# A fused attention and maxout kernel: the first quad by halves, one engine's copies, other stores, a new mask list and a new instruction order

## The chip, the cores and the metric

The kernel runs on one core of a Trainium2 chip. Five engines work on their own instruction streams, each in order, and wait for one another by semaphores: TensorE (PE, matrix products and transposes; its weight loads are shown apart as PEld), VectorE (DVE), ScalarE (ACT), GpSimd (POOL) and SyncE (SP), which here only issues transfers. Sixteen DMA engines carry them out. The metric is the device time of one execution in microseconds, the median of several runs; lower is better.

## What is computed

Inputs: q, k and v of 8 batches x 8 heads x 576 tokens x 64, three weights of 512 x 768 and one of 768 x 512, all float32. Only scores within tau = 0.02 of the row's maximum take part in the softmax.

```
scores = q @ k.T / sqrt(64)                       # 576 x 576 for each of 64 heads
scores = where(scores >= max(scores) - tau, scores, -1e9)
attn   = exp(scores - max(scores));  attn /= sum(attn) + 1e-9
x      = (attn @ v), heads side by side           # 4608 x 512
h      = maximum(x @ w1, x @ w2, x @ w3)          # 4608 x 768
out    = h @ w_out                                # 4608 x 512
```

## The kernel before

**Quads.** Four heads of one batch make a quad g (16 of them), held as two pairs r = 0, 1 of two heads i = 0, 1. `load` (line 181) fetches q and k with head i on partitions 64i to 64i+63, 9 tokens to a partition: the first eight tokens of both pairs in one transfer and the ninth ones in another, then v in four transfers. For the first quad alone (`first=True`) the eight-token rows come apart by pair: q on SP's queue in three transfers (pair 0, ninth tokens, pair 1), k likewise on ACT's queue. All other loads are on SP's.

**Transposes.** `transposed` (257) turns q or k of one pair on PE, ten 64 x 64 pieces for r = 0 (with the ninth tokens) and eight for r = 1, for both heads at once, into a PSUM slot. `evacuated` (234) copies the slot to `qt` (ACT, with the scale) or `kt` (DVE; ACT for pair 1 of the first quad). `swapped` (242) makes `qs`, a copy of `qt` with the partition halves exchanged, on POOL (for the first quad one of the two halves on DVE), so that both halves of PE's rows can work on the same queries.

**Scores.** A step is a quad and one of 9 chunks idx of 128 queries; each has a score product (S) for r = 0 and 1. Chunks 0 to 3 belong to head i = 0 of each pair, 5 to 8 to head 1, and chunk 4 holds the last 64 queries of both. Each S fills one of four PSUM slots, which are shared by all of PE's products.

**Softmax in two ways.** `maximum` (311) is a DVE pass that gives the row's bound. If the list `MASKED` has a 1 for the step and pair, this pass also writes z, ACT exponentiates once, and DVE removes what is under the threshold and sums (`numerators`, 331, letter k). With a 0, ACT runs twice over the scores (a Prelu with the tiny slope 2^-100, then an exponential that sums, letter n) and DVE has the maximum only. So a 1 costs DVE a pass, a 0 costs ACT one. Then DVE takes reciprocals, POOL normalizes to bf16 (`P`), and SP's queue transposes P by DMA into `ptq`.

**Products and the network.** `product` (358) multiplies `ptq` by v for one pair into `xt`; its 576 columns are copied by DVE for r = 0 and for r = 1 by ACT (512) and DVE (64). Once a batch has both its quads, `ffn` (426) runs 18 hidden products (each in two halves, F and B), of which ACT copies the first of three (`hm`) and DVE takes two maxima (`hm`, `hT`), and then the output products: two of 2 x 512 columns and one for the ninth tokens. ACT copies these to `ob` and `obr`, SP stores them. Batch 7 is done in two column parts (`SPLIT`).

**The order.** What is issued when is written out by hand in the text `ORDER`, which the loop at line 659 reads: S, T, O, F and a slot number issue PE's score products, transposes, attention products and the first halves of the network's products; B the second halves; m, e, k, n, r, p, t the maximum, exponent, the two kinds of numerators, reciprocal, normalization and DMA transpose of the next score in line; a and c the copies to `qt` and `kt`, q the swaps, x and w the copies of attention products by ACT and DVE, h, v and u those of the network; l a transfer of the next quad, y a POOL cast of v, g a load and z a cast of weights, o a store. `_Ordered` (80) ties every instruction to the one before it on its engine, so the text is each engine's order, and a wait holds back all that follows on that engine. Before the text is read, 12 warm-up transposes of the identity run on PE, and the first quad is loaded, transposed and swapped (lines 546 to 556).

## Time and profile before

| what | value |
|---|---|
| median of 3 runs | 452.66 us (452.27 to 452.84) |
| profiled execution, its own time | 451.11 us |
| its span, first to last instruction | 449.3 us |
| mean granted clock of TensorE | 0.991 |
| PE, DVE, ACT, POOL busy | 425.6, 402.0, 392.3, 314.8 us |
| chain that ended last: PE, DVE, POOL, DMA, ACT | 75%, 6%, 5%, 5%, 3% |
| first score product, first maximum | 8.08, 9.56 us |
| first network product | 67.39 us |
| last ob copy, last store issue begins | 444.29, 446.3 us |

The span leaves out 1.8 us that lie around the instructions. The profile gives for each engine the time in which it executed something; PE's is flattered, since matmuls overlap and their ends are modelled. Nearly all instructions carry line 89, the helper of `_Ordered`, so groups are told apart by the names of their tiles.

### The profile page before, as it was taken

Reading aid. Unit: us, or ns where it says so; the run is one execution under the profiler, and the core shown is the slowest. Engines: PE = TensorE matmul, PEld = TensorE weight load, DVE = VectorE, ACT = ScalarE, POOL = GpSimd, SP = SyncE. Lnnn points to the kernel's source line nnn. Section 1 sums busy time; section 2 is a strip of 40 time slices with the busy share of each in tenths; the row PEclk is TensorE's granted clock in tenths of the full one; section 3 lists DMA queues with packets and bytes.
Section 4 is the critical chain, followed back from the end, with each engine's and each line's share of the span. In section 5 each row is a group of like instructions: output and inputs, shape, how many; then the busy total and the mean of one; then the engine's idle time right before and its main releaser. Section 6 shows DMA issues by size and latency. Waiting matters only on the chain.

```text
span 449.3 us, 14063 instructions
## 1 busy us (share of the span) xinstructions
PE 425.6 (95%) x5188; PEld 314.8 (70%) x5188; DVE 402.0 (89%) x1115; ACT 392.3 (87%) x794; POOL 314.8 (70%) x416
## 2 busy tenths in 40 slices
PE   6766889999999999999999999999999999999995
PEld 6433557767688768878677867868787787787762
DVE  3999999998999999999989999999999999999541
ACT  3999999999899999999989999999999999866422
POOL 3798889989795985586776785659777787534400
PEclk8989999999999999999999999999999999999999
DMA  8989999999999999996999998999999999546622
GB/s 236 276 208 204 223 214 226 222 231 222 246 212 193 214 221 231 192 222 132 221 166 194 236 217 182 215 229 216 200 172 186 213 175 191 107 77 133 130 94 107
DMA packets 212773, 87.44 MB, mean 195 GB/s; under 512 B 185824, under 2 KB 199648, under 8 KB 212704
## 3 DMA queue, kind: packets, MB, share of 16 engines
q1 hardware_dynamic: 212144, 85.95, 93.4%
q8 instruction: 41, 0.67, 0.6%
q10 hardware_dynamic: 560, 0.59, 0.5%
q14 instruction: 28, 0.23, 0.2%
HBM read 34.60 MB, written 9.44 MB: 98 GB/s over the span
## 4 chain that ended last, share of the span: by engine, by line
PE 75%; DVE 6%; POOL 5%; DMA 5%; ACT 3%; issue 3%; SPq 1%; ACTq 0%; POOLq 0%; DVEq 0%
PE ph L89 30%; PE sc L89 26%; PE po L89 8%; PE o L89 8%; POOL P L89 3%; PE tp L89 3%; DVE z L89 3%; DVE unused L89 2%; ACT z L89 2%; DMA ptq<-P 1%; SPq L89 1%; DMA qm<-in_q_dram 1%; DMA km<-in_k_dram 1%; POOL qs L89 1%; ACT ob L89 1%
## 5 line engine op out<-in xcount | busy, mean ns | idle before, releaser
L89 POOL TENSOR_SCALAR P<-z,rs 128x576 bf16<-128x576 f32 x288 | 229.2, 811 | 89.4 <-DVE rs L89 40.6
L89 PE MATMUL sc<-kt,qs 64*128 64x256 f32 (+2 forms) x640 | 180.2, 421 | 9.2 <-ACT qt L89 3.2
L89 PE MATMUL sc<-kt,qt 64*128 64x320 f32 (+2 forms) x640 | 181.2, 432 | 4.0 <-DVE kt L89 1.2
L89 PE MATMUL ph<-xt,w 64*128 64x288 bf16 (+2 forms) x2160 | 165.0, 283 | 0.3 <-DVE hm L89 0.2
L89 PEld LDWEIGHTS <-w 64*128 64x128 bf16 (+1 forms) x2160 | 127.1, 94 | 29.4 <-issue 6.7
L89 ACT ACTIVATE z<-sc,nm 128x576 f32<-128x576 f32 x179 | 128.8, 742 | 11.6 <-DVE unused L89 9.7
L89 DVE TENSOR_SCALAR_CACHE_REDUCE unused<-sc 128x576 bf16<-128x576 f32 x179 | 130.3, 751 | 4.0 <-PE sc L89 3.4
L89 ACT ACTIVATE z<-z 128x576 f32<-128x576 f32 x179 | 121.0, 682 | 0.1
L89 PEld LDWEIGHTS sc<-kt,qs 64*128 64x128 f32 (+1 forms) x640 | 91.5, 178 | 33.3 <-ACT z L89 7.8
L89 PEld LDWEIGHTS sc<-kt,qt 64*128 64x128 f32 (+1 forms) x640 | 91.6, 177 | 21.0 <-ACT z L89 6.5
L89 DVE SCALAR_TENSOR_TENSOR z<-z 128x576 f32<-128x576 f32 x109 | 89.9, 839 | 0.3 <-ACT z L89 0.2
L89 DVE TENSOR_SCALAR_CACHE_REDUCE z<-sc 128x576 f32<-128x576 f32 x109 | 80.6, 752 | 7.4 <-PE sc L89 3.6
L89 ACT ACTIVATE z<-z,nm 128x576 f32<-128x576 f32 x109 | 81.8, 774 | 4.0 <-DVE z L89 3.4
L89 POOL COPY qs<-qt 64x640 f32<-64x640 f32 (+1 forms) x62 | 45.4, 733 | 14.7 <-ACT qt L89 11.6
L89 PE MATMUL po<-wo,hT 64*128 64x512 bf16 (+1 forms) x480 | 54.0, 356 | 0.1
L89 DVE TENSOR_TENSOR hm<-ph,hm 128x576 bf16<-128x576 f32 (+2 forms) x54 | 37.1, 687 | 12.1 <-PE ph L89 11.6
L89 ACT ACTIVATE hm<-ph 128x576 bf16<-128x576 f32 (+2 forms) x54 | 32.1, 595 | 14.9 <-PE ph L89 14.4
L89 PEld LDWEIGHTS <-hT 64*128 64x128 bf16 (+1 forms) x480 | 29.6, 97 | 16.7 <-issue 3.1
L89 DVE TENSOR_TENSOR hT<-ph,hm 128x576 bf16<-128x576 f32 (+2 forms) x54 | 37.2, 688 | 2.8
L89 PE MATMUL o<-ptq,vb 128*64 128x64 bf16 (+2 forms) x544 | 38.9, 281 | 0.2
L89 ACT ACTIVATION_READ_ACCUMULATOR z<-z 128x1 f32 x179 | 35.7, 199 | 0.0
L89 PEld LDWEIGHTS <-vb 128*64 128x64 bf16 x544 | 23.7, 111 | 14.2 <-issue 4.6
(32 smaller groups left out, 273.8 us busy)
## 6 DMA issues: line engine op xcount, KB each, us to landing
vm<-in_v_dram SPq DMA_DIRECT2D x32, 256.0 KB, 4.5
out_dram<-ob SPq DMA_DIRECT2D x32, 256.0 KB, 2.8
qm<-in_q_dram SPq DMA_DIRECT2D x15, 512.0 KB, 4.9
km<-in_k_dram SPq DMA_DIRECT2D x15, 512.0 KB, 4.7
stage<-in_moe_w_dram SPq DMA_DIRECT2D x9, 512.0 KB, 4.6
ptq<-P SPq DMA_TRANSPOSE x144, 4.1
stage<-in_moe_w_out_dram SPq DMA_DIRECT2D x3, 512.0 KB, 5.8
qm<-in_q_dram SPq DMA_DIRECT2D x16, 64.0 KB, 3.1
```

The costliest lines, as they stand in the source:

```text
L89: ins = fn(*a, **kw)
```

## The change

- The first quad is loaded by halves of the partitions: rows 0 to 63 (head 0 of each pair) first, in three transfers each of q (SP) and k (ACT's queue), the ninth tokens ahead of the rest; then rows 64 to 127, in two transfers each of q and k, all on SP. Before the text is read only head 0 is transposed, copied and swapped; the halves of head 1 become the first four T of the text, with their own a, c and q. Two filler transposes of the identity are put behind the first pair's k, and there is a thirteenth warm-up.
- In the first quad the copy of pair 1's k goes from ACT to DVE, and all swaps to POOL; the swaps are issued after the four transposes.
- `product`: for r = 1 ACT copies all 576 columns; DVE has no part in it.
- In the last batch the ninth tokens' products are copied by DVE instead of ACT, and the second store of the last 2 x 512 columns is issued on ACT's queue instead of SP's.
- `MASKED` has 102 ones of 288 instead of 109: by batch 11, 12, 11, 12, 12, 13, 12, 19, where there were 14, 9, 13, 15, 14, 13, 12, 19.
- `ORDER` is another text throughout. The number of each letter is the same but for what follows from the above: T 64 (60), a and c 32 (30), q 64 (60), k 102 (109), n 186 (179), w 16 (30). The first lines of both texts and the rest of the diff:

```diff
--- before.py
+++ after.py
@@ -22,51 +22,52 @@
 FLAT = 2.0 ** -100
 
 MASKED = """
-101000100110000110011100001010010001100010001000101000010000100000100010
-000011110101100001001001001001000001011100101011000110001010010000010011
-001010011101100000101100100001001010000110011111000001000100000110000101
-001001001101100000110001000100101000001100010011100101110110000001111111
+010000100100100010101001001100000010100011011001010000011000100000010100
+000110010101100001000011000001000010001100011010011000100000010101000100
+000111101000100010010010000100010001000110000101010100110100001101000100
+100111100100100010010000001100100000001001011110000011011110010101111100
 """
 
 
-WARM = 12
+WARM = 13
+FILL = (2, 0)
 SLOTS = 4
 SPLIT = (7,)
 ZBUFS = 4
 PBUFS = 6
 
 ORDER = """
-glllllS0lylS1mylyeS2zmlkS3lelmnlT0mS1aS2rmeqS0meqmeS3pnkT1pT0nrcaptemS0yeS1mgS2eympeS3mqtnT1S0mqnS2knrceprmS
-1epkepeS3mnyS0rkptemnS2pmnlzmS3erremtpT0empS1eklpaS2kgnS0ptnmeprrmlS1epS3mleS2pmlS0eplmetpmeS1knS3tkernkS2pt
...
+S0S1gmlS2elmgnyS3mlelT0ymeylT1kezlS2arclnT3mlnS0S1lzameT3lmeqgqrcnlT2plnpaqT1leS0qcplS3mpS2lrmT1eplmaqT0eklS
+1qnS2lmS3lepmteymeS1keqS3rnmpS2emprS1tepmnkqS3ncnprmS0elprmS1epS2megpkS0ntzS3nmntrmpemS2pemepS1kezetrmS0nmS3
...
 """
 
 
@@ -180,7 +181,7 @@
 
     def load(g, first=False):
         b, qd = quads[g]
-        L = Ls[g] = dict(b=b, qd=qd, first=first)
+        L = Ls[g] = dict(b=b, qd=qd)
         for n in "qk":
 
             L[n] = ld.tile([128, 20, D], F32, name=n + "m")
@@ -188,20 +189,28 @@
         def rows_of(src):
             return src[b, 4 * qd:4 * qd + 4].rearrange("(r i) (p c) d -> (i p) r c d", r=2, c=9)
 
-        q2 = nc.scalar if first else sync
-        srcs = (("q", q, sync), ("k", k, q2))
         if first:
-            for n, src, e in srcs:
-                e.dma_start(out=L[n][:, 0:8], in_=rows_of(src)[:, 0, 0:8])
-        for n, src, e in srcs:
-            e.dma_start(out=L[n][:, 8:10], in_=rows_of(src)[:, :, 8])
-            yield
-        for n, src, e in srcs:
-            if first:
-                e.dma_start(out=L[n][:, 10:18], in_=rows_of(src)[:, 1, 0:8])
-            else:
-                e.dma_start(out=L[n].rearrange("p (r c) d -> p r c d", r=2)[:, :, 0:8], in_=rows_of(src)[:, :, 0:8])
-            yield
+
+            for i in range(2):
+                rows = slice(64 * i, 64 * i + 64)
+                srcs = (("q", q, sync), ("k", k, sync if i else nc.scalar))
+                for n, src, e in srcs:
+                    e.dma_start(out=L[n][rows, 8:10], in_=rows_of(src)[rows, :, 8])
+                if i == 0:
+                    for r in range(2):
+                        for n, src, e in srcs:
+                            e.dma_start(out=L[n][rows, 10 * r:10 * r + 8], in_=rows_of(src)[rows, r, 0:8])
+                else:
+                    for n, src, e in srcs:
+                        e.dma_start(out=L[n].rearrange("p (r c) d -> p r c d", r=2)[rows, :, 0:8],
+                                    in_=rows_of(src)[rows, :, 0:8])
+        else:
+            for n, src in (("q", q), ("k", k)):
+                sync.dma_start(out=L[n][:, 8:10], in_=rows_of(src)[:, :, 8])
+                yield
+            for n, src in (("q", q), ("k", k)):
+                sync.dma_start(out=L[n].rearrange("p (r c) d -> p r c d", r=2)[:, :, 0:8], in_=rows_of(src)[:, :, 0:8])
+                yield
         L["vm"] = ld.tile([128, 4, 4, D], F32, name="vm")
         L["vr"] = ld.tile([128, 2, D], F32, name="vr")
         vsrc = v[b, 4 * qd:4 * qd + 4].rearrange("h (p c) d -> p h (c d)", c=9)
@@ -234,18 +243,15 @@
     def evacuated(L, n, r, dst, src):
         if n == "q":
             scalar.activation(out=dst(L["qt"]), in_=src, func=AF.Copy, scale=scale)
-        elif L["first"] and r == 1:
-            scalar.activation(out=dst(L["kt"]), in_=src, func=AF.Copy)
         else:
             vector.tensor_copy(out=dst(L["kt"]), in_=src)
 
-    def swapped(L, r):
+    def swapped(L, r, ii=(0, 1)):
 
         cols = slice(320 * r, 320 * r + 64 * (5 - r))
-        for x in range(2):
-            e = vector if x == 1 and L["first"] else pool
-            e.tensor_copy(out=L["qs"][64 * x:64 * x + 64, :, cols],
-                             in_=L["qt"][64 - 64 * x:128 - 64 * x, :, cols])
+        for x in (0, 1) if len(ii) == 2 else (1, 0):
+            pool.tensor_copy(out=L["qs"][64 * x:64 * x + 64, ii[0]:ii[-1] + 1, cols],
+                             in_=L["qt"][64 - 64 * x:128 - 64 * x, ii[0]:ii[-1] + 1, cols])
             yield
 
     def targets(L, n):
@@ -254,7 +260,7 @@
             if n == "q":
                 L["qs"] = qk.tile([128, 2, S], F32, name="qs")
 
-    def transposed(L, n, r):
+    def transposed(L, n, r, ii=(0, 1)):
 
 
         st = {}
@@ -264,7 +270,7 @@
             st["ps"] = ps = bank("tp", where)
             main = ps.rearrange("p (i z) -> p i z", i=2)[:, :, 0:256].rearrange("p i (jj u x) -> p i jj x u", jj=2, x=2)
             for j in range(nj):
-                for i in (1, 0):
+                for i in ii[::-1]:
                     rows = slice(64 * i, 64 * i + 64)
                     tensor.transpose(main[:, i, j // 2, j % 2] if j < 4 else ps[:, 512 * i + 256:512 * i + 320],
                                      couple(L, n, r, j, rows), identf[rows, rows])
@@ -272,8 +278,8 @@
         def done():
             targets(L, n)
             off = 320 * r
-            evacuated(L, n, r, lambda t: t[:, :, off:off + 64 * nj],
-                      st["ps"].rearrange("p (i z) -> p i z", i=2)[:, :, 0:64 * nj])
+            evacuated(L, n, r, lambda t: t[:, ii[0]:ii[-1] + 1, off:off + 64 * nj],
+                      st["ps"].rearrange("p (i z) -> p i z", i=2)[:, ii[0]:ii[-1] + 1, 0:64 * nj])
         return _Piece((L["b"], L["qd"], n, r), first, None, [done])
 
     def scores(L, idx, r, where):
@@ -379,10 +385,8 @@
         def on_vector():
             ps = st["ps"]
             dst = target(L["b"])[:, 2 * L["qd"] + r, :]
-            if part is None and r == 0:
+            if part is None:
                 vector.tensor_copy(out=dst, in_=ps[:, 0:S])
-            elif part is None:
-                vector.tensor_copy(out=dst[:, 512:S], in_=ps[:, 512:S])
             else:
                 vector.tensor_copy(out=dst[:, 256:S], in_=ps[:, 0:320])
 
@@ -390,13 +394,13 @@
             ps = st["ps"]
             dst = target(L["b"])[:, 2 * L["qd"] + r, :]
             if part is None:
-                scalar.activation(out=dst[:, 0:512], in_=ps[:, 0:512], func=AF.Copy)
+                scalar.activation(out=dst, in_=ps[:, 0:S], func=AF.Copy)
             elif part == 1:
                 scalar.activation(out=dst[:, 0:256], in_=ps[:, 0:256], func=AF.Copy)
             else:
                 scalar.activation(out=dst[:, 256:S], in_=ps[:, 0:320], func=AF.Copy)
         p = _Piece((L["b"], L["qd"], r, part), first)
-        p.vector = on_vector if part is None or part == 2 and r == 0 else None
+        p.vector = on_vector if part != 1 and r == 0 else None
         p.scalar = on_scalar if part == 1 or r == 1 else None
         return p
 
@@ -480,8 +484,10 @@
 
             def done(a):
                 ob = hp_.tile([128, DM], F32, name="ob", bufs=4)
+                last = a == 1 and c == 2 and b == B - 1
                 scalar.activation(out=ob, in_=my["ps"][:, 512 * a:512 * a + 512], func=AF.Copy)
-                stores.append(lambda: sync.dma_start(out=rows_out[:, (0, 2, 1, 3)[c + a]:8:4], in_=ob))
+                e = scalar if last else sync
+                stores.append(lambda: e.dma_start(out=rows_out[:, (0, 2, 1, 3)[c + a]:8:4], in_=ob))
             p = _Piece((b, "out", c), first, lambda: my["h"][1](), [lambda: done(0), lambda: done(1)])
             p.kind = "u"
             return p
@@ -499,7 +505,10 @@
 
             def done():
                 ob = hp_.tile([128, DM // 2], F32, name="obr", bufs=2)
-                scalar.activation(out=ob, in_=my["ps"][:, :256], func=AF.Copy)
+                if b == B - 1:
+                    vector.tensor_copy(out=ob, in_=my["ps"][:, :256])
+                else:
+                    scalar.activation(out=ob, in_=my["ps"][:, :256], func=AF.Copy)
 
                 def store():
                     for x in range(2):
@@ -548,12 +557,14 @@
     for _ in load(0, first=True):
         pass
     for x, (r, n) in enumerate(((0, "q"), (0, "k"), (1, "q"), (1, "k"))):
-        p = transposed(Ls[0], n, r)
-        p.first(x)
+        p = transposed(Ls[0], n, r, (0,))
+        p.first(x % 3)
         p.done[0]()
-        if n == "q":
-            for _ in swapped(Ls[0], r):
-                pass
+        if n == "k":
+            for _ in range(FILL[r]):
+                tensor.transpose(warm[:, 0:128], identf, identf)
+    for _ in zip(*(swapped(Ls[0], r, (0,)) for r in range(2))):
+        pass
 
 
     def chunks():
@@ -584,7 +595,7 @@
 
     made, pending = [], []
     todo = dict(S=((c, r) for c in chunks() for r in range(2)),
-                T=((g, n, r) for g in range(1, NQ) for r in range(2) for n in "qk"),
+                T=((g, n, r) for g in range(NQ) for r in range(2) for n in "qk"),
                 O=products(), F=pieces())
     line = {k: [] for k in "menkrptahvuxwcq"}
     casts = iter([w[1] for w in wl])
@@ -600,9 +611,10 @@
             line["m"].append((c, r))
         elif what == "T":
             g, n, r = next(todo["T"])
-            p = transposed(Ls[g], n, r)
+            ii = (0, 1) if g else (1,)
+            p = transposed(Ls[g], n, r, ii)
             p.first(where)
-            line["a" if n == "q" else "c"].append((p, g, r))
+            line["a" if n == "q" else "c"].append((p, g, r, ii))
         elif what == "O":
             p = next(todo["O"])
             p.first(where)
@@ -643,10 +655,10 @@
         elif what == "t":
             turned(line["t"].pop(0))
         elif what in "ac":
-            p, g, r = line[what].pop(0)
+            p, g, r, ii = line[what].pop(0)
             p.done[0]()
             if what == "a":
-                line["q"].append((Ls[g], r))
+                line["q"].append((Ls[g], r, ii))
         elif what in "hvuxw":
             line[what].pop(0)()
         elif what in "pqyl":
```

More of the change, by code (lines that the diff above doesn't have):

```diff
@@ new lines @@
+nmS0npmF3geF2ymtBerkBphF0lrnS1vlqS3nmF2pemBpteBvzeT1rS0chpS3nmF2ptnmF1qBekBpeF0vnS3rtnBvpS2mhzS1grmS0epmT2eg
+pS3mtaF1pmeF2qkBetBeF0vnS3rknBpS1vhznrmF0S2mepBmeyS1tyvS3qemF0npgF2mpeBrkBzeT1vhS3ncT2pgS0arrtmS1pnO2mpemtye
+T3weS0pcnS2pmS1nlF3prmnF0zmeBlBevtqS1ekpO2nvlnqrmlS3xpS0mgeF2ptmeS1prBkepF3thS0mnF2zmeBrBezvtS1nS0vpnS3rpF2m
+tnpmnS1pmetBmpeerktpS0eS3muyS1lrpmuS0ekplF2elmnlpmS3noS1yrmpBnlpemleO3klekluO1rlkuponwT0oxprT2rT3atcS1paS0mp
+eF2lmqS3etBkqeS1mhF0qmF2epBeT3yvBnF1tvnyS0qcBnyS2tmhyS3meF1pmlF0eBorkepF2lvnBlBpnvS3tnrS1pmhF0mpteBrrS2epvS3
@@ new lines @@
+nymS1pnF0mpT2emBpatS3veyS2mS0elmeS1rmepF3lmepF2lkBeT0lhkBtnF1vF3nrcBptnS2vynT0BmatS1prrhS2mpeF0tmS3peBmepS1l
+vS2qelkO0nqlmnlO3pnmtqewqT2nrrS1tcpxS0meF2pF3meBeBvT1hT0klT2aF3caS1qntS2pmF0nrpBmetBpvnS2qS1nvtS3qemF0prmeF2
+ptmeykyeT1BlknpncS3urrtS1upmuS0pmeS2lpmeS1opS3meF0rmepomeqlS1kS2eplBlmnonmS3lerkplO2nktepO1umnlywS3ulrS2xpmt
+S0epmF1emyBeF3keF2rkhBpS0nvtS1npmBnF3mlS0evBterrrS2mphF1mpeF3tkBpeBvntF0pnS2vBpnmtS1phrS3mepS0moeS2ptmeF1meS
+0leBmlT3nvT2lF0actS1nF3rmpeBtkBpeS2vhS1nrmS3pF0mtepF2meBqBtevF1nkF3nT0vBaBrkphT2S0ncF1pmnF2qBvteBqrrvS3hqS0m
@@ new lines @@
+npS1rmS2epO3meptmepO0keptwS1xpS2nlmF3tnrmF0peBrpBevS1ynyS2lvnF3mlynpS0rmluS1pemoT3S2pemtF0epmayklS1etkS3eBmn
+rmpelS2klpeF1lmulukS3eoS0rmnpBkteprnmS2S3yulmuO0mlqeoepO1wtnqreprT2T0xcS3ptaS1mnF2qkF0eqBmBthyrS3pevS1pnF2tm
+F0pmeBpBtevF3phkF1ynlT2BcnyF0rvnS2lpBrmlS3pvlBepoS2mhF1ptmeF0kBeBtvnT3S2rnvpS1oampF0tS3meqBmeS2lrepS1mlhpS3m
+leS0qmleF2mteF3kF1eBktnBvnBS0rnvpS2nmpO3hmetS1weF0rnrmT3pT2nBcpS1avptS3nmT2peO0mqetcqeS1rpxS2mF3npmS0etBknF2
+veT1BrrmapS3hF1pmeS2kqteBF0mnS3yvleqBrmT1nlypF2cnpS3evS1ptumS0npmF2etrmepS3kepS1lnrS0mlpnBmoepmoeS3kuS0muF1o
```

43 lines of the change are left out of this document (14 added, 29 removed).

## The prediction

> **What bounds it now.** I read the page's busy shares and slices first, then busy time by stretches, the timeline of the first 15 us, the groups by form, and the last stores. The profiled execution took 451.11 us around a span of 449.3 us; the median of the runs is 452.66 us. I sum on the span and add to the median.
>
> ```profile
> PE 425.6 (95%) x5188; PEld 314.8 (70%) x5188; DVE 402.0 (89%) x1115; ACT 392.3 (87%) x794; POOL 314.8 (70%) x416
> PE   6766889999999999999999999999999999999995
> PEclk8989999999999999999999999999999999999999
> ```
>
> TensorE (PE) is full except at both ends. Stretches (busy us of PE, PEld, DVE, ACT, POOL, then clock):
>
> ```profile
> 15.00:20.00 5.00, 3.48 (x46) 1.86 (x42) 4.90 (x15) 5.00 (x11) 4.86 (x7) 1.00 0.88 266
> 30.00:40.00 10.00, 6.14 (x46) 2.88 (x44) 9.44 (x31) 9.94 (x20) 8.43 (x10) 1.00 0.99 195
> 40.00:80.00 40.00, 34.21 (x385) 22.85 (x387) 38.22 (x109) 39.03 (x83) 36.74 (x47) 1.00 1.07 223
> ...
> 120.00:280.00 160.00, 159.70 (x2061) 121.52 (x2059) 153.44 (x425) 150.22 (x301) 119.00 (x159) 1.00 1.03 204
> 280.00:360.00 80.00, 80.00 (x1057) 62.13 (x1053) 76.44 (x213) 77.69 (x160) 58.37 (x79) 1.00 1.02 205
> ```
>
> So there are three stages. Up to 80 us there are mostly scores to compute, and VectorE (DVE) and ScalarE (ACT) are the wall; PE idles 13.1 us between 15 and 80. From 80 to 440 us PE is the wall, with DVE and ACT at 94 to 97%. Last come the stores. A gain must come from an earlier start, from a shorter end, or from PE waits inside the first 80 us. The matmuls stay the same, apart from one warm-up and two filler transposes.
>
> The start, in order of time:
>
> ```profile
> 5.17 0.64 PE L89 MATMUL tp<-identf,qm 64*128 64x64 f32 x10 [0.99 <-DMA qm<-in_q_dram]
> 6.71 0.95 POOL L89 COPY qs<-qt 64x640 f32<-64x640 f32 x1 [5.40 <-ACT qt L89]
> 6.88 0.47 PE L89 MATMUL tp<-identf,qm 64*128 64x64 f32 x8 [0.75 <-DMA qm<-in_q_dram]
> 8.08 0.76 PE L89 MATMUL sc<-kt,qs 64*128 64x256 f32 x1 [0.48 <-ACT qt L89]
> 9.56 0.76 DVE L89 TENSOR_SCALAR_CACHE_REDUCE z<-sc 128x576 f32<-128x576 f32 x1 [1.12 <-PE sc L89]
> 13.23 0.53 PE L89 MATMUL tp<-identf,qm 64*128 64x64 f32 x10 [1.34 <-DMA qm<-in_q_dram]
> ```
>
> The transposes wait for loads twice, at 5.17 and 6.88 us; the first maximum, where the wall of the first stage begins, starts at 9.56 us. At 13.23 PE waits for the second quad's load.
>
> **Start, part one: the first maximum.** Now 64 KB + 256 KB each of q and k (640 KB) are moved for the first transposes and 512 KB for the second. With rows 0 to 63 alone it is 320 KB and 256 KB. The load rate around 4 us is about 387 GB/s in the DMA view, so 576 KB less is 1.5 us less: the third load, still third in its queue, lands at 5.4 instead of 6.88. The first pair's load is 0.8 us shorter but goes out second, one issue (0.48 us) later: 4.85 instead of 5.17. Thirteen warm-ups at 0.235 end at 4.4, so PE idles 0.45 instead of 0.99. From 4.85, half transposes (0.35), a half ACT copy (the 640-wide takes 0.70; half about 0.45) and a half POOL swap (0.95 at full width; half about 0.5) put the first score at about 6.3. Score to maximum took 1.48 us at the first score, where the granted clock was 0.50, but 0.83 us at 13.56, clock 1.00. I take 0.9, since in the 3 us before the score PE would now have little idle: first maximum at 7.2, 2.3 us earlier. Bounds: if half a load takes as long as a whole one, it is 9.5, a gain of nothing; with all at the full rate and POOL proportional, 6.8, 2.7 us.
>
> **Start, part two: what is left of the lead.** The order puts the four transposes of the second heads behind scores 4, 4, 5 and 7, and the second quad's first two, which were behind scores 4 and 8, behind score 7: PE is in order, so score 8, and all behind it, waits for the second quad's keys. Their load is issued at 8.47 now and landed 6.4 us later, at 14.9. SP's queue has four more half loads ahead of it (4 x 0.48 us) and the second weight piece (0.59 us, 512 KB, 1.3 us at 387 GB/s). By bytes it is 14.9 + 1.3 = 16.2, by issue times with the same 6.4 us 17.4. I take 16.2, as the DMA engines are full in this stretch (share 0.98 to 1.03), so bytes decide. By then DVE, from 7.2 us, has done 7 maxima at 0.68 (their pitch), a 0.83 numerator, two reciprocals and two half key copies (0.45 each), 6.8 us in all, and stands idle from 14.0: a first maximum up to 2.2 us later would cost it nothing. The old DVE at 16.2 has done the numerator and two thirds of the seventh maximum (from 15.75). The lead on DVE is the last third and a reciprocal, 0.4 us. ACT's is one exponent more and four of the second ones at 0.67, less what the old one does up to 16.2: 2.9 us, partly because the new list masks fewer steps (the 36 bits of batch 0 hold 14 ones now, 11 after), which moves work from DVE to ACT. Both engines being the wall, I value it between the two, somewhat under their mean of 1.6: **1.3 us**. The half copies' fixed part is in it, and so are the first swaps, now POOL's alone: DVE's 0.49 and 0.42 go to it, 4 halves of 0.5, against its 5.4 us of idle before 6.71. Bounds: -0.9 (keys at 17.4, DVE then most of a numerator behind) and 2.1 (keys at 15.5, half of their extra bytes hidden; the leads then 0.8 and 3.3).
>
> **First 80 us after that.** Counting letters up to the twentieth F: 84 scores before, 83 after; maxima 83 and 81, exponents 81 and 80, DVE numerators 25 and 25, ACT ones 53 and 52, six h and twelve v in both, and 16 against 18 whole T. Neither is ahead: 0. Bounds: 13.1 us of PE idle lie here; a better order might win half, a worse one lose as much as DVE's 1.8 us wait now at its largest.
>
> **Middle: mask and copies.**
>
> ```profile
> L89 DVE SCALAR_TENSOR_TENSOR z<-z 128x576 f32<-128x576 f32 x109 | 89.9, 839 | 0.3 <-ACT z L89 0.2
> L89 ACT ACTIVATE z<-z 128x576 f32<-128x576 f32 x179 | 121.0, 682 | 0.1
> L89 ACT ACTIVATE xt<-o 128x512 bf16<-128x512 f32 x14 | 8.3, 596 | 1.5 <-DVE xt L89 0.7 <-PE o L89 0.3
> L89 DVE CAST xt<-o 128x64 bf16<-128x64 f32 x14 | 3.1, 219 | 2.8 <-ACT xt L89 2.5 <-PE o L89 0.2
> ```
>
> Masked steps go from 109 to 102: DVE loses 7 x 0.839 = 5.9 us, ACT gains 7 x (0.742 + 0.682 - 0.774) = 4.6 us. The 14 odd heads' copies drop DVE's 0.219 each (3.1 us) and its waits for ACT's half; ACT's grow from 512 to 576 columns, 0.596 to about 0.648 (the 576-wide hm copy), 0.7 us. DVE thus falls from 402.0 to about 393, ACT rises to about 397.6. Neither is on the chain while PE is full: 0. Cover gone, ACT's 5.3 us would show (a rival below).
>
> **End.**
>
> ```profile
> 444.77 0.39 ACT L89 ACTIVATE obr<-po 128x256 f32<-128x256 f32 x1
> 445.70 1.20 SPq L89 DMA_DIRECT2D out_dram<-obr  x2
> ```
>
> SP's last four issues start at 444.42, 445.06, 445.70 and 446.3; a landing and the fixed close follow. The store of the second ob moves to ACT's queue, where only the end of that engine's work is behind it, and the ninth's copy to DVE, idle since 440.13: its matmuls end near 444.5, the 256-wide DVE pass takes 0.42, so the two obr issues can start at 445.06. One issue of **0.6 us** leaves the chain; 0 if the moved 256 KB still occupies the DMA engines ahead of them (0.7 us at 390 GB/s), 0.7 at most.
>
> Sum: 1.3 + 0 + 0 + 0.6 = 1.9 us, span 447.4, median **450.7**.
>
> **Rivals.** (A) *The lead dies at the loads*: half loads gain less, the second quad's keys land at 17.4, and DVE is 0.9 behind; with the end's 0.6 it is +0.3, 453.0. For it: SP issues without a pause from 4.93 to 11.95, and every issue added shifts the rest; against it: the DMA engines, not SP, are full. [...]
>
> (B) *ACT becomes the wall in the middle* (slower). From 120 to 280 us ACT is at 150.2 of 160; the masks removed between scores 84 and 215 (52 before, 46 after up to score 219, so about 7) add 4.6, the copies 0.5: 155.3, or 97.1%. If ACT, in order and coupled to PE through four PSUM slots, can be filled only to 94.9% as in 80 to 120 (37.94 of 40), the stretch takes 163.6, 3.6 us more: net +1.7, 454.4. It decides from a ceiling below 95.9%, where 1.9 us are eaten. Against it: 280 to 360 us ran with ACT at 97.1% and PE at 80.00 of 80, and DVE's relief of 9 us loosens the other side.
>
> (C) *The order also fills PE in the first 80 us*: half of the 13.1 us of idle, less the shared lead of 1.3: 1.9 + 5.2 = 7.1, 445.6. For it: DVE loses work and the swaps come sooner; against: the counts up to the twentieth F.
>
> **Chances.** Forecast 0.50, own range 449.2 to 452.1; A 0.17; B 0.21; C 0.12. A measurement of this kernel tells some 0.2% (0.9 us) from no change, that is below 451.75 or above 453.57. Faster: 0.43 of the forecast, C's 0.12, 0.04 of A, together 0.59. Same: 0.07 and 0.10 of A, 0.17. Slower: B and 0.03 of A, 0.24. The range, 447.2 to 454.2, leaves out the far part of C and of B.
>
> **What would show it.** First maximum near 7.2 with clock 1.0 in the scores after it; transposes of the second quad waiting for its km until about 16.2, with DVE idle from 14; F number one at or before 67.4, where it is now; PE full from 80; ACT's share of 120 to 280 near 97%; the two obr issues following the first ob's directly, 0.6 us earlier against the last matmul. I am wrong if the second quad's keys come after 17, or PE shows new waits for ACT after 100 us.

## The result

The kernel became slower: 457.81 us in the median (455.63 to 458.88) against 452.47 us for the kernel before on the same chip (451.68 to 452.84), a ratio of 1.0114 with a 95% interval of 1.0073 to 1.0156. That is 5.3 us more, where 1.9 us less were predicted, and outside the range. The profiled execution took 457.27 us around a span of 455.5 us (before: 451.11 and 449.3), so 6.2 us are to be found in it.

The page of the changed kernel, busy time and PE's row of slices:

```profile
PE 427.0 (94%) x5191; PEld 316.5 (69%) x5191; DVE 396.4 (87%) x1089; ACT 397.0 (87%) x808; POOL 316.4 (69%) x422
PE   7675889989999999999999999999999999999996
```

DVE fell by 5.6 us and ACT rose by 4.7 us, where 9 and 5.3 were worked out. PE's slices hold a 9 from the seventh on, as before, but for the ninth (91 to 102 us), which holds an 8; beyond that a loss of 1% doesn't show in tenths. Busy time by stretches (PE, PEld, DVE, ACT, POOL, then granted clock, DMA share, GB/s):

```profile
15.00:20.00 5.00, 2.14 (x28) 1.59 (x27) 1.49 (x5) 3.73 (x8) 3.79 (x6) 0.88 1.09 351
...
40.00:80.00 40.00, 33.30 (x370) 23.72 (x368) 37.75 (x106) 38.00 (x80) 34.98 (x44) 0.91 0.98 193
80.00:120.00 40.00, 37.18 (x438) 26.46 (x432) 36.24 (x96) 36.95 (x77) 33.95 (x44) 1.00 1.08 203
120.00:280.00 160.00, 158.39 (x2033) 118.86 (x2035) 148.81 (x410) 153.62 (x314) 119.52 (x159) 1.00 1.00 207
280.00:360.00 80.00, 80.00 (x1047) 59.98 (x1045) 75.17 (x209) 76.37 (x154) 57.44 (x76) 1.00 0.99 203
```

The same row of the kernel before, from 80 to 120 us:

```profile
80.00:120.00 40.00, 39.51 (x469) 27.92 (x467) 37.51 (x105) 37.94 (x80) 33.88 (x44) 1.00 1.16 227
```

From 15 to 20 us DVE works 1.49 us, where it worked 4.90: 3.4 us are gone at one place. From 80 to 280 us PE idles 4.4 us of 200, where it idled 0.5 from 80 to 120 and 0.3 from 120 to 280. From 280 to 360 us PE idles nothing. By events: the twelfth maximum comes 3.9 us later than before (25.10 against 21.19), the 36th also 3.9, the 60th 6.1, the last hm copy 6.5, the end 6.2. The marks in the middle hold the order of the text as well as its lateness: the same text with the old start (r1_oldstart below) is 3.4 us behind before at the 60th maximum and 1.7 us ahead at the 84th.

The start in the timeline (start, duration, engine, what; in brackets the idle time before it and what ended it):

```profile
5.18 0.52 PE L90 MATMUL tp<-identf,qm 64*128 64x64 f32 x5 [0.79 <-DMA qm<-in_q_dram]
...
6.41 0.46 PE L90 MATMUL tp<-identf,qm 64*128 64x64 f32 x4
...
7.73 0.45 PE L90 MATMUL sc<-kt,qs 64*128 64x256 f32 x1 [0.61 <-DVE kt L90]
...
8.58 0.76 DVE L90 TENSOR_SCALAR_CACHE_REDUCE unused<-sc 128x576 bf16<-128x576 f32 x1 [0.99 <-PE sc L90]
...
17.30 0.53 PE L90 MATMUL tp<-identf,qm 64*128 64x64 f32 x10 [2.01 <-DMA qm<-in_q_dram]
...
18.67 0.76 PE L90 MATMUL tp<-identf,km 64*128 64x64 f32 x10 [0.84 <-DMA km<-in_k_dram]
...
19.47 0.82 DVE L90 COPY kt<-tp 128x640 f32<-128x640 f32 x1 [3.51 <-PE tp L90]
```

In this execution the first maximum is 1.0 us earlier than before, not 2.3, and the new start did not bring even that, as the last section shows. Then PE waits twice for the second quad's load, and DVE stands for 3.51 us until that quad's keys can be copied. The chain of work that leads there (start, duration, what) is a chain of SP's issues from 0.73 to 11.09 us with pauses of 0.06 us at most, and then one transfer, which lands at 18.53:

```profile
10.58 0.51 SPq L90
...
11.12 7.41 DMA km<-in_k_dram
```

The last stores of the changed kernel, for the predicted 0.6 us:

```profile
451.07 0.42 DVE L90 COPY obr<-po 128x256 f32<-128x256 f32 x1 [4.40 <-DMA out_dram<-ob]
451.46 0.64 ACTq L90 DMA_DIRECT2D out_dram<-ob  x1
451.60 1.42 SPq L90 DMA_DIRECT2D out_dram<-obr  x2
```

From the start of the last hm copy to the end of the span it is now 10.5 us, 0.4 less than before (10.9).

### The profile page after: what moved, and what is told of

Read it like the earlier page. It is cut to its first block, busy times and chain, and to the rows that moved or that the text cites. A ratio compares the mean times of both kernels' runs of the same rounds, so it can differ in the third digit from the quotient of the medians.

```text
span 455.5 us, 14097 instructions
## 1 busy us (share of the span) xinstructions
PE 427.0 (94%) x5191; PEld 316.5 (69%) x5191; DVE 396.4 (87%) x1089; ACT 397.0 (87%) x808; POOL 316.4 (69%) x422
## 4 chain that ended last, share of the span: by engine, by line
PE 69%; POOL 6%; DVE 6%; issue 5%; ACT 5%; DMA 5%; SPq 2%; DVEq 0%; POOLq 0%; ACTq 0%
PE ph L90 25%; PE sc L90 24%; PE po L90 9%; PE o L90 8%; ACT z L90 4%; POOL P L90 4%; DVE z L90 3%; DMA km<-in_k_dram 3%; PE tp L90 3%; SPq L90 2%; DVE unused L90 2%; POOL qs L90 1%; DMA stage<-in_moe_w_dram 1%; POOL w L90 1%; DMA out_dram<-ob 1%
## 5 line engine op out<-in xcount | busy, mean ns | idle before, releaser
L90 PEld LDWEIGHTS <-w 64*128 64x128 bf16 (+1 forms) x2160 | 128.9, 94 | 29.4 <-issue 5.5
L90 DVE TENSOR_SCALAR_CACHE_REDUCE unused<-sc 128x576 bf16<-128x576 f32 x186 | 135.5, 751 | 9.2 <-PE sc L90 7.7
L90 ACT ACTIVATE z<-sc,nm 128x576 f32<-128x576 f32 x186 | 132.7, 739 | 11.5 <-DVE unused L90 7.1
L90 ACT ACTIVATE z<-z 128x576 f32<-128x576 f32 x186 | 125.4, 680 | 0.2
L90 DVE SCALAR_TENSOR_TENSOR z<-z 128x576 f32<-128x576 f32 x102 | 84.8, 847 | 0.2 <-ACT z L90 0.2
L90 DVE TENSOR_SCALAR_CACHE_REDUCE z<-sc 128x576 f32<-128x576 f32 x102 | 75.4, 750 | 7.6 <-POOL P L90 4.4
L90 ACT ACTIVATE z<-z,nm 128x576 f32<-128x576 f32 x102 | 77.4, 772 | 4.8 <-DVE z L90 4.3
L90 POOL COPY qs<-qt 64x640 f32<-64x640 f32 (+3 forms) x68 | 48.1, 708 | 14.3 <-ACT qt L90 8.8
L90 PEld LDWEIGHTS <-hT 64*128 64x128 bf16 (+1 forms) x480 | 30.8, 97 | 16.4 <-issue 2.7
L90 DVE COPY kt<-tp 128x640 f32<-128x640 f32 (+3 forms) x34 | 24.3, 716 | 11.5 <-PE tp L90 11.3
```

The source lines that it names most:

```text
L90: ins = fn(*a, **kw)
```

## The experiments

All ratios are against the kernel before, run on the same chip in the same session (medians 451.6 to 452.9); runs of different sessions are compared by these ratios. One per cent is 4.5 us.

**The start out of the change, and the start alone.** r1_oldstart is the changed kernel with whole loads and both heads before the text; r2_newstart is the kernel before with the new start alone.

```diff
 # r1_oldstart: the loads, transposes, copies and swaps of the first quad as before
-WARM = 13
+WARM = 12
-S0S1gmlS2elmgnyS3mlelT0ymeylT1kezlS2arclnT3mlnS0S1lzameT3lmeqgqrcnl
+S0S1gmlS2elmgnyS3mlelymeylkezlS2rlnmlnS0S1lzmelmegrnl
 # r2_newstart: the text of before, with the second heads ahead of its first T
-glllllS0lylS1mylyeS2zmlkS3lelmnlT0mS1aS2rm
+glllllS0lylS1mylyeS2zmlkS3lelmnlT0T1acqqT0T1acqqT0mS1aS2rm
```

> The changed kernel with the start of before: the first quad loaded by whole partitions in six transfers, transposed, copied and swapped for both heads ahead of the text (DVE's swap and ACT's copy of pair 1's k included), twelve warm-ups; the text's first four T with their a, c and q left out. Theory 1 (the start: second quad's keys land at 18.5 instead of 14.9 us and DVE stands 3.5 us): the wait goes, some 4 of the 5.3 us come back, 452.5 to 454. Theory 2 (the new text and mask list cost it all along, the start little): 456 or more.

> The kernel of before with the new start alone: loads by halves, head 0 first, warm-ups and fillers; the old text, with the four transposes of the second heads and their copies and swaps put in ahead of its first T; old masks, copies and stores. Theory 1: first maximum near 8.6 us, but the second quad's keys come 2 us or more later (no second weight piece is ahead of them in the old text, so not all 3.6); 454 to 456. Theory 2: within 1 us of before, 451.5 to 453.5.

Measured: r1_oldstart 454.47 us, 1.0051 (1.0028 to 1.0074); r2_newstart 457.16, 1.0114 (1.0084 to 1.0143). The new start alone costs as much as the whole change. But the changed kernel with the old start is slower than before too, so there are two losses, and they don't add up simply.

r1_oldstart's profile shows what the start does to the same text. Its first score products take as long as the changed kernel's, and its first maximum comes at the same time:

```profile
7.99 0.38 PE L90 MATMUL sc<-kt,qs 64*128 64x256 f32 x1
...
8.55 0.76 DVE L90 TENSOR_SCALAR_CACHE_REDUCE unused<-sc 128x576 bf16<-128x576 f32 x1
...
16.65 0.52 PE L90 MATMUL tp<-identf,km 64*128 64x64 f32 x10 [0.84 <-DMA km<-in_k_dram]
...
17.21 0.82 DVE L90 COPY kt<-tp 128x640 f32<-128x640 f32 x1 [1.93 <-PE tp L90]
```

PE waits for the second quad's keys here too, but they are there 2 us earlier, DVE stands 1.93 us instead of 3.51, and the twelfth maximum comes at 21.63 us instead of 25.10. Its text is also without the four transposes of the second heads and their copies, so not all of these 3.5 us belong to the load.

**One weight piece moved.** r3_weight_behind moves the second g and its z behind the second quad's loads.

```diff
-S0S1gmlS2elmgnyS3mlelT0ymeylT1kezlS2arclnT3mlnS0S1lzameT3lmeqgqrcnlT2plnpaq
+S0S1gmlS2elmnyS3mlelgT0ymeylT1kezlS2arclnT3mlnS0S1lameT3lmeqgqrcnlT2plnpzaq
```

> The changed kernel with one letter g (the second weight piece, 512 KB) put behind the four transfers of the second quad's q and k, and its cast z behind the second p. Theory 1: the keys land 1.5 to 2 us earlier, near 16.8, DVE's wait of 3.5 us shrinks to some 1.7, and the time falls by 1.5 to 2, to about 456. Theory 2: no difference beyond 0.5 us.

Measured: 457.27 us, 1.0114 (1.0083 to 1.0145). In its profile the eighth maximum is at 19.06 instead of 20.60, but DVE is then busy for only 17.2 of the 20 us from 20 to 40. The second quad's transposes no longer wait for a load: they start at 17.43 and 17.80 us, where they started at 17.30 and 18.67 after waits of 2.01 and 0.84. The time is the same as the changed kernel's, so this run does not show the wait for these keys as the price. In this execution the first maximum came only at 10.51 us, 1.9 later than in the changed kernel's, and by the 36th maximum (54.73 against 54.54) the gain was gone; whether the piece costs nothing or its gain is given back, the run doesn't tell.

**The loads by whole partitions.** r7_whole keeps the new start by heads but loads the first quad in three transfers of q (SP) and three of k (ACT's queue), ninth tokens first. r10_newstart_whole does the same to r2_newstart.

```diff
-            for i in range(2):
-                rows = slice(64 * i, 64 * i + 64)
...
+            srcs = (("q", q, sync), ("k", k, nc.scalar))
+            for n, src, e in srcs:
+                e.dma_start(out=L[n][:, 8:10], in_=rows_of(src)[:, :, 8])
+            for r in range(2):
+                for n, src, e in srcs:
+                    e.dma_start(out=L[n][:, 10 * r:10 * r + 8], in_=rows_of(src)[:, r, 0:8])
```

> The changed kernel with the first quad loaded by whole partitions, three transfers of q on SP and three of k on ACT's queue, ninth tokens first: four issues fewer on SP. The rest as changed, so head 0 is still transposed first. Theory 1 (SP's longer chain of issues is what makes the second quad late): the keys land near 15.5, first maximum 9 to 9.5, the time falls by 2 to 3, to 454.5 to 455.5. A variant, that the half transfers only land slower: the same first maximum or an earlier one, at 8.6 or below. Theory 2: no difference beyond 0.5 us.

> r2_newstart (old text with the new start) with the first quad loaded by whole partitions, three transfers of q on SP and three of k on ACT's queue. If half transfers are what costs, as the step from the changed kernel to r7_whole says (2.2 us), the time falls from 457.2 to about 455; if the late transposes of the second heads in PE's order are, it stays at 456.5 to 457.5.

Measured: r7_whole 455.53 us, 1.0065 (1.0041 to 1.0090), against 1.0114 with half loads; r10_newstart_whole 453.36, 1.0026 (1.0007 to 1.0046), against 1.0114. In the old text the half loads cost 0.9% (4 us) with the same bytes, and the intervals are far apart. In the new text the difference is 0.5% (2.2 us), with intervals that overlap, and the same step with one more load moved (r12_after_late_q and r13_whole_late_q below) gives 1.0148 against 1.0134, nothing; so there it is not shown. Both steps change two things, the width of the loads and the four more issues on SP's queue, and no run separates them. The stretches from 5 to 8 us of the changed kernel:

```profile
5.00:6.00 1.00, 0.82 (x11) 0.75 (x11) 0.00 (x0) 0.26 (x1) 0.00 (x0) 1.00 0.79 125
6.00:7.00 1.00, 0.97 (x11) 0.72 (x10) 0.49 (x1) 0.27 (x2) 0.44 (x1) 1.00 0.77 254
7.00:8.00 1.00, 0.39 (x4) 0.30 (x4) 0.42 (x1) 0.29 (x1) 0.59 (x2) 1.00 1.05 230
```

and of r7_whole:

```profile
5.00:6.00 1.00, 0.28 (x3) 0.29 (x4) 0.00 (x0) 0.00 (x0) 0.00 (x0) 1.00 1.06 366
6.00:7.00 1.00, 1.00 (x11) 0.88 (x10) 0.00 (x0) 0.44 (x1) 0.00 (x0) 1.00 1.04 374
7.00:8.00 1.00, 1.00 (x7) 0.67 (x7) 0.49 (x1) 0.00 (x0) 0.44 (x1) 1.00 1.06 322
```

The last column is the rate: 125 to 254 GB/s with half loads, 322 to 374 with whole ones; the loads of v are in these stretches too, so these are rates of mixtures. In the rows at 5 and 6 us of the changed kernel the share of busy DMA engines is 0.79 and 0.77, so a part of the low rate is engines that were not busy. In the row at 7 us the share of busy DMA engines, the column before it, is the same in both (1.05 and 1.06), and the rate is 230 against 322. SP's queue in the changed kernel adds to it:

```profile
0.73 2.96 SPq L90 DMA_DIRECT2D qm<-in_q_dram  x4
3.73 0.62 SPq L90 DMA_DIRECT2D km<-in_k_dram  x1
```

A half load of q or k takes 0.60 to 0.83 us to issue (2.96 for the first four), a whole one 0.41 to 0.51 (1.45 for three before). Seven half loads of the first quad stand in this queue where three whole ones stood, and the second quad's last k is issued at 11.12 us instead of 8.47.

**The mask list.** r6_masks is the kernel before with seven masked steps of batches 1 to 4 unmasked, the letter k turned into n where it stands; r9_more_masked is r1_oldstart with seven steps masked, n turned into k.

```diff
 # r6_masks, one of seven places
-eT1pBrteBkyhS2cpn
+eT1pBrteBnyhS2cpn
 # r9_more_masked, one of seven
-BerkBphF0lrnS1vlqS3nmF2pem
+BerkBphF0lrnS1vlqS3kmF2pem
```

> The kernel of before with seven masked steps of batches 1 to 4 made unmasked (102 ones, as many as in the change), their letters k turned to n in place; nothing else. Theory 2a (ScalarE is the wall from 80 to 280 us; PE's weight loads wait 11 us for it there in the changed kernel, 5.4 us before): ACT gains 4.6 us there, the time grows by 1 to 2.5 us. Theory 2b (the count of masked steps doesn't matter, the new text's order does): within 0.5 us of before.

> The changed kernel with the old start (as in r1_oldstart) and seven unmasked steps of batches 1 to 4 made masked (109 ones), n turned to k in place. Theory 2a: ACT's load falls by 4.6 us and the time by 1 to 2.5 us against r1_oldstart, to 452 to 453.5. Theory 2b: no gain, 454 to 455, or a loss, as the text was made for the other list.

Measured: r6_masks 456.65 us, 1.0091 (1.0066 to 1.0116); r9_more_masked 460.68, 1.0182 (1.0156 to 1.0208), where r1_oldstart had 1.0051. Taking seven passes from DVE and giving ACT 4.6 us more, by the prediction's sum, costs 4 us in the old text; doing the opposite in the new text costs 6 us. ACT's load alone therefore doesn't decide. That a list and a text belong together, and that after either change the letters around it come at moments when their inputs aren't there, is my reading; no run shows which letters wait.

**Copies and stores alone.** r5_copies is the kernel before with the odd heads' copies by ACT alone; r4_tail is the kernel before with the new end alone.

```diff
 # r5_copies
-                vector.tensor_copy(out=dst[:, 512:S], in_=ps[:, 512:S])
-                scalar.activation(out=dst[:, 0:512], in_=ps[:, 0:512], func=AF.Copy)
+                scalar.activation(out=dst, in_=ps[:, 0:S], func=AF.Copy)
 # r4_tail
-                stores.append(lambda: sync.dma_start(
+                e = scalar if last else sync
+                stores.append(lambda: e.dma_start(
...
+                if b == B - 1:
+                    vector.tensor_copy(out=ob, in_=my["ps"][:, :256])
...
-uooBF1uuouoo
+uooBF1uuuooo
```

> The kernel of before with the odd heads' products copied by ScalarE alone, all 576 columns, and their letters w left out. By the sum DVE loses 14 x 0.219 us and ACT gains 14 x 0.05: within 0.5 us of before under both theories; a gain of up to 1 us if DVE's waits for ACT's half (2.5 us in all) were on the chain; a loss of about 1 us if ACT is the wall and each copy starts late.

> The kernel of before with the last stores spread: the last batch's ninth tokens copied by DVE and the last ob stored from ACT's queue, last six letters uuuooo. In the changed kernel's profile the last hidden product's copy to the end of the span took 0.3 us less than before: a gain of 0.3 to 0.6 us.

Measured: r5_copies 452.44 us, 1.0006 (0.9985 to 1.0027), nothing; r4_tail 451.30, 0.9982 (0.9965 to 0.9999), 0.8 us faster. r4_tail is the one version here whose interval lies below the kernel before, by a hair.

**Which part of the new text loses.** Three hybrids with the old start and the new end: h1_old_new84 has the old text and list up to score 84 and the new ones after it; h2_new_old84 the reverse; h3_new_old187 the new ones up to score 187 and the old ones after.

```diff
 # MASKED of h1_old_new84, its first 84 bits from before, the rest from after
-010000100100100010101001001100000010100011011001010000011000100000010100
+101000100110000110011100001010010001100010001000101000010000100000100010
-000110010101100001000011000001000010001100011010011000100000010101000100
+000011110101100001000011000001000010001100011010011000100000010101000100
...
```

> Old start; the old text and mask list up to score 84 (near 116 us), the new text, mask list and tail from there; odd heads copied by ACT alone throughout. In the profile of r1_oldstart the 84th maximum is 1.7 us ahead of before and the end 6 us behind. Theory 3 (the new text is better up to there and loses all of its cost after it): 454 to 456, as slow as r1_oldstart or slower. Theory 4 (the loss is already in the state at score 84 or spread evenly): 452.5 to 453.5.

> Old start; the new text and mask list up to score 84, the old ones from there, with the new tail; odd heads copied by ACT alone. Theory 3: the front's 1.7 us and the tail's 0.8 us are kept: 449.5 to 450.5, faster than both kernels. Theory 4: no gain over before, 451.5 to 453.5.

> Old start; the new text and mask list up to score 187 (near 260 us), the old ones from there, with the new tail. Tells where after score 84 the new text loses: all between 84 and 187 gives 453.5 to 455, all after 187 gives 450 to 451.5.

Measured: 455.13 us, 1.0067 (1.0043 to 1.0090); 455.55, 1.0084 (1.0058 to 1.0110); 452.57, 1.0020 (1.0001 to 1.0039). Neither half at score 84 can be named as the one that loses: both hybrids come out no better than the whole new text (1.0051), with intervals that overlap its own. In the profile of h2_new_old84 the 84th maximum is 1.9 us behind the kernel before and the 100th 7.3, so the seam itself seems to cost 5 us. Only h3_new_old187 is readable: in its profile the new text up to score 187 has lost 1.95 us at the 200th maximum, and under the old text the lag does not grow any more. Against r1_oldstart it is 0.3% better, so the new text seems to lose again after score 187, but the two intervals overlap.

**The wait at 300 us.** r1_oldstart's profile shows what happens there. POOL and PE in its timeline:

```profile
290.16 1.91 POOL L90 COPY qs<-qt 64x640 f32<-64x640 f32 x2 [2.05 <-DVE rs L90]
...
292.16 4.34 POOL L90 TENSOR_SCALAR P<-z,rs 128x576 bf16<-128x576 f32 x6
...
300.87 1.12 PE L90 MATMUL o<-ptq,vb 128*64 128x512 bf16 x14 [2.16 <-DMA ptq<-P]
```

and its stretch:

```profile
280.00:320.00 40.00, 37.84 (x494) 29.66 (x492) 34.55 (x94) 33.13 (x67) 28.68 (x38) 0.96 1.01 181
```

Two swaps stand ahead of six normalizations on POOL; POOL idles 2.05 us before them, by the row until a reciprocal of DVE (rs), and they take 1.91 us. The normalizations follow in one burst, the transposes of P land late, PE waits 2.16 us for one and its granted clock falls to 0.96 in the mean of the stretch. My first trial moved one load of 512 KB behind two transposes, in r1_oldstart (r11), in the changed kernel (r12) and in r7_whole (r13). The expectations call it q's; the issues show that it is k's, issued at 273.28 us in r1_oldstart and at 279.25 in r11_late_q.

```diff
-peT2klpS0atS3mnS2eBrmptempeS3qeO0muknO2wtuk
+peT2kpS0atS3mnS2eBrmptlempeS3qeO0muknO2wtuk
```

> The changed kernel with the old start, as in r1_oldstart, and one letter of the text moved: the load of 512 KB of q that stands ahead of the last two DMA transposes of the products at 300 us is issued behind them. Theory 4 (in some executions of the new text a transpose of P lands late, behind that load, so that the attention product at 300 us waits 2.2 us and the clock falls to half for 3.4 us; that is what spreads r1_oldstart from 452.9 to 456.6): no wait of the product for ptq in the profile, the highest time under 455.3, the median 453.2 to 453.6 (r1_oldstart 454.47). Rival (the wait is a sign of DMA engines that are full there, and the load behind only moves it; or it is too rare to count): median within 454.0 to 455.0, highest again at 456.

> The changed kernel with that one letter moved and nothing else. Theory 4: what its wait at 300 us costs goes from the executions that have it: 456.4 to 457.0 against 457.8, the highest under 458. Rival: PE comes to the product 3 us later than in r1_oldstart and has no such wait, so nothing changes: 457.3 to 458.1.

> The changed kernel with the first quad loaded by whole partitions, as in r7_whole, and that one letter moved. Theory 4: its profile had the same wait of 2.2 us and r7_whole went from 454.3 to 458.5; now 454.2 to 454.8 in the median and under 456.5 at the highest, and TensorE's idle time from 200 to 440 us falls from 2.3 us to under 0.5. Rival: 455.2 to 455.9.

Measured: 455.01 us, 1.0072 (1.0047 to 1.0097); 458.83, 1.0148 (1.0122 to 1.0174); 458.15, 1.0134 (1.0101 to 1.0167). The theory fell, and the trial was aimed badly: counting the products shows that this load stands ahead of the pair at 276 us, not of the one at 300, and the wait at 300 us is still in the profiles of r11 (1.8 us), r12 (1.5 us) and r13 (2.5 us). What the runs do show is that one load moved by seventeen letters can cost 0.7% (r13 against r7_whole, whose intervals are apart); in r11 and r12 the same move stays within the intervals. The second trial moves the two swaps behind the six normalizations, in r1_oldstart (r14) and in the changed kernel (r15):

```diff
-F2rvBqlBtkqhS1nrvT0F3npmF2npBcBptvS0hprrS3mepS2tmeS1pmeS3ytF0m
+F2rvBlBtkhS1nrvT0F3npmF2npBcBptvS0hprrS3mepS2tmeS1pqqmeS3ytF0m
```

> The changed kernel with the old start, as in r1_oldstart, and two letters of the text moved: the two swaps of the next quad's q that stand ahead of six normalizations are issued behind them. In r1_oldstart's trace POOL is idle for 2.05 us ahead of these swaps (290.16), the six normalizations run only from 292.16, the transposes of P follow, and the product at 300.9 waits 2.16 us for one. Theory 5 (POOL's order, not the loads, makes that wait; the next quad's scores come only after 305 us, so that the swaps can wait): normalizations from about 290.2, no wait of the product at 300 us, TensorE's idle time from 280 to 320 us from 2.2 us to under 0.3, the highest time under 455.3 and the median 452.6 to 453.5 (r1_oldstart 454.47). Rival (any letter moved costs as much as it gives, as with the load in r11_late_q): 454.2 to 455.2.

> The changed kernel with these two swaps moved and nothing else. Theory 5: where an execution has the wait at 300 us it goes: 455.8 to 457.0 in the median against 457.8, highest under 458. Rival: its profile had no such wait, so 457.3 to 458.3.

r14_late_swap's stretch:

```profile
280.00:320.00 40.00, 40.00 (x538) 31.89 (x540) 38.73 (x105) 36.93 (x74) 31.79 (x43) 1.00 0.95 193
```

The wait is gone, PE is busy for 40.00 of 40 and the clock is 1.00, so it hung on POOL's order in this text. POOL's idle time did not go: it stands 2.19 us before the normalizations, which start at 291.45, not at the expected 290.2. What the move gave is the swaps' 1.9 us. In the time it is worth less than expected: r14_late_swap 454.14 us, 1.0035 (1.0014 to 1.0057) against r1_oldstart's 1.0051, a difference within the intervals; r15_after_late_swap 459.37, 1.0133 (1.0098 to 1.0168), no gain over the changed kernel's 1.0114. The wait is in the profiled execution of r1_oldstart, the slowest of its ten, and not in that of the changed kernel, whose POOL has the same order and the same 2.05 us.

The pairs of this section tell about the start as well, since each has the same text with the new and the old start: r12 against r11 is 1.0148 against 1.0072, and r15 against r14 is 1.0133 against 1.0035. In both the intervals are apart.

## Why the prediction was wrong

The runs give the terms of the sum as follows (positive is time lost; the predicted ones were -1.3, 0 and -0.6 us).

| term | predicted | measured | from |
|---|---|---|---|
| start | -1.3 us | +2.8 us | the change 1.0114, with the old start 1.0051 |
| text, mask list and copies | 0 | +3.1 us | r1_oldstart's 2.3 us with the end's 0.8 taken out |
| end | -0.6 us | -0.8 us | r4_tail |

They sum to 5.1 us, against 5.3 measured, but that is no test of the split: the terms are differences of the same ratios. For the start the two intervals overlap by a hair (one begins at 1.0073, the other ends at 1.0074); the pairs r12 and r11, r15 and r14 give 3.4 and 4.4 us for it with intervals apart, so the new start costs time in the new text too. In the old text it costs 5.2 us (r2_newstart).

**Start, part one** gave nothing, where 2.3 us were taken. The step moved 576 KB less at the rate of whole loads, 387 GB/s; in the stretches from 5 to 8 us the rate was 125 to 254. So the first transposes began at 5.18 and the second group at 6.41, where 4.85 and 5.4 were worked out. From the score to the maximum it was 0.85 us (0.9 predicted) at a granted clock of 1.00; that PE's little idle time before it keeps the clock up was my estimate, and no run isolates it. The first maximum came at 8.58, not 7.2, and r1_oldstart, with the old start and score products as short, has it at 8.55. The step measured its lead from a start whose first score products took 0.63 to 0.90 us, and the half loads did not even bring the first transposes sooner: they begin at 5.04 to 5.43 us in the five profiles with half loads and at 4.57 to 5.17 in the eleven with the old start. Half loads and whole loads stand as 125 to 254 against 322 to 374 GB/s, in stretches that hold other transfers too, and beside the DMA engines' share of 0.79 and 0.77 at 5 and 6 us no run shows what lowers the rate.

**Start, part two** is the step that failed with the most behind it: the start's term of -1.3 us became a loss of 2.8 to 4.4. It said that bytes decide, not SP's issues, because the DMA engines' share was near 1.0, and put the second quad's keys at 16.2 us. They were issued at 11.12 and landed at 18.53, so both bounds were too early (17.4 was the late one): the issues alone took 2.65 us more, and the landing 7.4 us where it had taken 6.4. This is past 17 us, which the prediction named as its sign of being wrong. A share near 1.0 did not mean the full rate, since it was 1.05 at 230 GB/s. The order's consequence was read rightly: score 8 and all behind it waits on PE, in order, for these keys, and DVE stood from 15.96 to 19.47. Its lead of 0.4 us became a lag of 3.9 at the twelfth maximum. Rival A named what this execution shows, at too low a price (+0.3 us in all). How much of the median hangs on it is open: r3_weight_behind has no wait for these keys in its profile and the same time, and r13_whole_late_q with whole loads is as slow as r12_after_late_q. That the loads by halves, with the issues that they add, make most of the new start's loss is shown in the old text alone (r10_newstart_whole).

**First 80 us and middle** were costed at nothing, since neither text was ahead in letter counts and DVE and ACT had slack while PE was full. With the old start the new text loses 0.5%. In its profile PE idles 2.3 us between 80 and 200 us, before 0.7; in those of r9_more_masked, r6_masks and the hybrids it idles 2.0 to 5.6 us there (in those of r4_tail and r5_copies, which keep the old text, 1.5 and 1.7, so part of it may be chance). Counting letters cannot see this, because it says how much each engine does and not whether an input is there when its letter comes. Rival B, ACT as the wall, has little for it: with less for ACT (r9_more_masked) the kernel got slower, and after 100 us PE waited 1.3 us for DVE's z, 0.8 for a load of keys and 0.2 for ACT in the changed kernel's profile. But r6_masks, with more for ACT, got slower too, so ACT's part is not excluded. One wait was traced to its cause (the swaps at 300 us), but it does not carry the median. Which of the small waits between 80 and 200 us make up the rest is open; the hybrids couldn't tell, as a seam costs more than what was looked for. Rival C is refuted by the row from 40 to 80 us: PE is busy for 33.30 us there, where it was for 34.21. In that stretch the granted clock was 0.91, before 1.00; the prediction had no term for it, and no run prices it.

**The copies** were nothing as predicted (r5_copies), and 0.649 us each on ACT where 0.648 was taken. The sum of ACT's work left out the read of its accumulator, 0.199 us with each of the seven scores that lost their mask, and that of DVE's work the first swaps, which leave it, and the copies of keys and of the last ninth tokens, which come to it; neither is a term of the time. **The end** was right, 0.8 us against 0.6, within what r4_tail's interval can tell.

## What to carry to other kernels

Splitting a load into halves of the partitions to have the first half sooner did not halve its time here: the rate fell by some 30% or more (125 to 254 GB/s against 322 to 374), each issue got longer (0.60 to 0.83 us against 0.41 to 0.51), and the first transposes began no sooner than with the old start's whole loads. Whole-width pieces cut along the tokens were the better split in one text (4 us) and not measurably so in the other. Before moving the first loads, follow the queue that issues them up to the next stage's load, since a few issues more can cost that stage more than the first one gains: here its last k was issued 2.65 us later. And where an order is written out by hand for one set of choices, a change of the choices (a mask list, a copy's engine) has to be tried as a pair with its order; busy shares and counts do not show what it will do.

## What was not expected of the hardware

The same start did not always run at the same speed. r2_newstart has the first transposes at the time of the changed kernel, 5.33 against 5.18 us, but its matmuls take longer:

```profile
9.49 0.63 PE L90 MATMUL sc<-kt,qs 64*128 64x256 f32 x1
...
10.41 0.76 DVE L90 TENSOR_SCALAR_CACHE_REDUCE z<-sc 128x576 f32<-128x576 f32 x1 [1.62 <-PE sc L90]
```

The same shape took 0.38 us at 8.02 us in the changed kernel:

```profile
8.02 0.38 PE L90 MATMUL sc<-kt,qs 64*128 64x256 f32 x1
```

With thirteen warm-ups in both, the first maximum came at 8.58 in one and 10.41 in the other. In the five profiles with half loads it lies between 8.55 and 10.51, in the eleven with the old start between 8.55 and 10.15, so up to 2 us of a start's lead is a matter of the execution, and one profile of each kernel cannot tell a lead of 1 us. That the clock makes the difference is likely but not shown. In the kernel before, this shape took the same 0.63 us where the granted clock was 0.50, from 8 to 11 us:

```profile
8.64 0.63 PE L89 MATMUL sc<-kt,qs 64*128 64x256 f32 x1
```

Yet for the rows of r2_newstart and of the changed kernel the profile gives a granted clock of 1.00, from 9 to 10 us in the one and from 8 to 9 in the other. The other surprise is how far executions of one kernel differ: 455.6 to 458.9 us for the changed kernel, 450.3 to 453.7 for the one before in a single session, both wider than most single steps of this prediction.
